# The first superchunk's inverse starts from the corners of its grams, and the second inverse moves behind the front

## The chip, the core and the metric

The kernel runs on one core of one Trainium2 chip. The metric is device time in microseconds, the median of several runs. A core has a matrix engine (TensorE, PE in the rows; PEld is its weight load), a vector engine (VectorE, DVE), an activation engine (ScalarE, ACT), a general engine (GpSimd, POOL) and a queue engine that starts transfers (SyncE, SP). Each works off its own list of instructions in order. They wait for each other by semaphores. SBUF is the memory on the core, PSUM the accumulator memory that TensorE writes, in banks of 128 x 2 KB.

## What is computed

A recurrent attention (delta rule) over 4 x 8 heads, 768 tokens and a head size of 48, and on its output two feed-forward layers, all in float32:

```python
k_n = k / (np.linalg.norm(k, axis=-1, keepdims=True) + 1e-06)
for t in range(768):
    y[:, :, t] = np.einsum('bhd,bhde->bhe', q[:, :, t], state)
    v_old = np.einsum('bhde,bhd->bhe', state, kt)
    state = state + bt[:, :, :, None] * np.einsum('bhd,bhe->bhde', kt, vt - v_old)
x = x @ w_a * (x @ w_b) @ w_out          # 3072 x 384, width 1536
h = x @ w_in                             # width 2048
y = (np.maximum(h, 0) + alpha * np.minimum(h, 0)) @ w_out2
```

## The kernel before

**Attention in chunks.** The 768 tokens are six superchunks of 128 tokens, each two steps (j = 0, 1) of 64. Within a step the recurrence is solved in closed form. The Gram matrix of the keys (`gram_keys`, tile `g`), scaled by b (beta and the key norms) and masked below the diagonal (`mask_keys`, into `ef`), gives a unit triangular 64 x 64 system for each of the 32 head columns of a step, and its inverse is needed. Each 64 x 64 system is cut into 32 x 32 blocks. The two diagonal blocks are inverted on DVE by substitution, all heads and both steps at once: `inverting` does it with 60 operations (a product into `itmp`, an addition into `inv`, 30 times), each pair depending on the pair before. `inverting_halves` does it with 88 operations by 16 x 16 blocks, and ACT hands blocks over between them. `diagonal` then transposes the result with two DVE transposes (`hw`, `TT`), and `offdiag` makes the block beside the diagonal with two sets of 32 x 32 matmuls on PE: `w`, whose results ACT copies into `hw`, and `xx`, whose results ACT copies into `TT`.

**A step.** `step` uses the inverse: `rp` (state times keys; v minus it on DVE), `up` (inverse times v, copied into SU), `sp` (the state's part, subtracted in SU on DVE) and `yp` (the output, which ACT and DVE split into the `x` of the feed-forward). `gram_queries` makes the masked query-key products that `yp` needs; before, ACT copies them out of PSUM (`keep_queries`) and POOL multiplies them with the mask (`mask_queries`). L is the superchunk at hand, N the next one.

**Feed-forward.** Its matmuls are 128 x 512 (3666 in all), float32 in three passes of a rounded format: `p` (up projections), `o` (down projection), and `h` and `o` of the second layer. For every pair of `p`, ACT copies one half out of PSUM (`a<-p`), DVE multiplies the other onto it (`a<-p,a`), ACT rounds it (`g<-a`) and POOL makes the remainder. Weights come as packed words and are decoded on DVE (`raw<-e`, `raw<-e,raw`), ACT (`e<-raw`, `W<-raw`, `wu<-W`) and POOL.

**What sets the order.** The program is recorded first, one operation after another; a list planner then writes the order of each engine from the dependencies, its table of costs and the order of recording. All instructions therefore bear one line, L201, and are told apart by tile names. In the front the attention of superchunk 0 (with the Gram matrices of superchunk 1) runs ahead of the first `p`. There the second inverse (of N) is recorded in small pieces: `early(n)` asks the weight decoding for a piece and, by `leisurely`, the second inverse for one whenever DVE is free. For c = 1 it is finished (`finish(inv)`) and followed by `diagonal` and `offdiag` between pieces of the feed-forward (`run(moe, ...)`). For c of 2 and more the inverse is made by `inverting_halves` at the end of the superchunk before.

## Time and profile before

| | us |
|---|---|
| median of 3 runs | 1021.15 (1020.98 to 1021.97) |
| span of the profiled execution | 1019.1 |
| PE busy in it | 977.5 (96%) |
| DVE, ACT, POOL busy | 610.0, 477.4, 574.7 |
| first big matmul `p` | 81.04 |
| the second superchunk's `rp` | 136.05 |

A timeline row gives the start, the length from the first to the last of a run of like instructions, the engine, the operation as output<-inputs with shapes, the number of instructions, and in brackets the idle time ahead of it with what ended it. A group row gives, behind the bar, busy time and the mean of one in ns, then the engine's idle time just before them. A small float32 matmul has two records in the trace (a set of 64 small matmuls reads x128), a 128x512 matmul one.

### The profile page before, as it was taken

What the parts mean: (1) busy time and instruction counts of PE and PEld (TensorE: products, weight loads), DVE (VectorE), ACT (ScalarE), POOL (GpSimd) and SP (SyncE); (2) the same over time, 40 slices, a digit from 0 to 9 for tenths busy, and PEclk for the clock granted to TensorE, in tenths of its full rate; (3) what the DMA queues carried; (4) which work ended last, traced back from release to release, by engine and by line L of the source; (5) the groups of instructions that cost most, each with busy time, mean ns of one, the idle gap of its engine ahead of it and who ended that gap; (6) DMA issues with size and microseconds to landing.
All of it is one profiled execution on the core that took longest, in us unless ns stands there. A gap on an engine that the chain in (4) does not pass through costs nothing.

```text
span 1019.1 us, 23984 instructions
## 1 busy us (share of the span) xinstructions
PE 977.5 (96%) x9950; PEld 805.1 (79%) x9950; DVE 610.0 (60%) x1232; ACT 477.4 (47%) x955; POOL 574.7 (56%) x512
## 2 busy tenths in 40 slices
...
GB/s 248 190 81 126 138 115 132 40 2 50 110 1 8 74 79 1 18 19 32 17 64 171 178 146 50 32 19 44 1 63 0 1 63 1 32 1 1 32 0 32
DMA packets 26940, 61.41 MB, mean 60 GB/s; under 512 B 4304, under 2 KB 8912, under 8 KB 26832
## 3 DMA queue, kind: packets, MB, share of 16 engines
q1 hardware_dynamic: 26400, 59.50, 19.3%
...
## 4 chain that ended last, share of the span: by engine, by line
PE 91%; DVE 5%; ACT 1%; issue 1%; DMA 1%; SPq 0%; DVEq 0%; POOL 0%; ACTq 0%
PE o L201 34%; PE p L201 29%; PE h L201 19%; PE up L201 2%; PE yp L201 2%; PE g L201 2%; DVE itmp L201 1%; DVE inv L201 1%; PE rp L201 1%; PE sp L201 1%; DMA k<-in_kn_dram 1%; PE xx L201 1%; PE w L201 1%; DVE raw L201 1%; DVE ef L201 0%
## 5 line engine op out<-in xcount | busy, mean ns | idle before, releaser
L201 PE MATMUL p<-x,wu 128*128 128x512 f32 x1296 | 318.0, 394 | 1.4 <-DVE x L201 0.7
L201 PEld LDWEIGHTS p<-x,wu 128*128 128x128 f32 x1296 | 240.2, 188 | 56.2 <-issue 2.4
L201 POOL TENSOR_TENSOR g<-neg,g 128x512 fp32r<-128x512 f32 x95 | 124.3, 1308 | 256.2 <-ACT g L201 255.6
L201 POOL TENSOR_TENSOR wu<-W,wu 128x384 fp32r<-128x384 f32 x195 | 200.3, 1033 | 110.6 <-ACT wu L201 109.0
L201 PE MATMUL h<-x,v 128*128 128x512 f32 x864 | 211.4, 389 | 0.0
L201 PE MATMUL o<-g,v 128*128 128x512 f32 x870 | 211.4, 388 | 0.0
L201 DVE TENSOR_SCALAR neg<-h,al 128x512 f32<-128x512 f32 (+1 forms) x97 | 72.2, 745 | 218.3 <-PE h L201 218.3
L201 ACT CAST g<-neg 128x512 fp32r<-128x512 f32 (+1 forms) x97 | 59.7, 616 | 298.8 <-DVE neg L201 277.3
L201 PEld LDWEIGHTS o<-g,v 128*128 128x128 f32 x870 | 162.5, 188 | 33.4
L201 PEld LDWEIGHTS h<-x,v 128*128 128x128 f32 x864 | 162.2, 188 | 33.7
L201 PE MATMUL o<-g,wu 128*128 128x512 f32 x648 | 165.5, 394 | 0.5 <-DVE TT L201 0.5
L201 ACT CAST wu<-W 128x384 fp32r<-128x384 f32 x216 | 109.9, 513 | 78.7 <-PE p L201 38.2
L201 PEld LDWEIGHTS o<-g,wu 128*128 128x128 f32 x648 | 120.0, 188 | 27.1 <-issue 0.9
L201 POOL TENSOR_TENSOR g<-a,g 128x512 fp32r<-128x512 f32 x71 | 93.3, 1314 | 30.3 <-ACT g L201 30.1
L201 PE MATMUL g<-Z 48*64 48x64 f32 (+1 forms) x1024 | 66.4, 275 | 27.9 <-DVE ef L201 17.9
L201 DVE TENSOR_TENSOR a<-p,a 128x512 f32<-128x512 f32 x72 | 49.3, 685 | 49.8 <-PE p L201 22.4
L201 DVE TENSOR_TENSOR inv<-inv,itmp 128x240 f32<-128x240 f32 (+23 forms) x236 | 69.9, 296 | 10.4 <-ACT eu L201 2.8
L201 PEld LDWEIGHTS g<-Z 48*64 48x64 f32 x1024 | 50.6, 160 | 28.9 <-DVE ef L201 18.2
L201 DVE SCALAR_TENSOR_TENSOR neg<-h,neg 128x512 f32<-128x512 f32 (+1 forms) x97 | 66.5, 686 | 3.3
L201 ACT COPY a<-p 128x512 f32<-128x512 f32 x72 | 42.2, 586 | 44.7 <-PE p L201 41.6
L201 ACT CAST g<-a 128x512 fp32r<-128x512 f32 x72 | 44.7, 620 | 22.5 <-DVE a L201 22.0
L201 POOL TENSOR_TENSOR f<-f,v 128x384 int32<-128x384 int32 x32 | 38.2, 1205 | 6.6 <-DVE v L201 4.0
...
## 6 DMA issues: line engine op xcount, KB each, us to landing
...
```

Of the source, the lines that this page charges most:

```text
L201: getattr(s.engines[op.eng], op.name)(*(real(x) for x in op.a), **{w: real(x) for w, x in op.k.items()})
```

## The change

For superchunk 0, `corners` makes only the 32 x 32 diagonal corners of the key grams, 128 small matmuls into two banks. DVE masks them with a constant (`corner`, -1 above the diagonal, made by POOL at the start) and transposes them into `turned`. `inverting_corners` multiplies by the transposed b in two halves straight into the PSUM room of the inverse, ACT copies each half to SBUF, and the 60 operations follow as before (`substituting`). `sides` makes the blocks beside the diagonal with 64 matmuls; ACT copies them out with the sign, POOL multiplies by b. `first_sides` takes the place of `diagonal` and `offdiag` for superchunk 0: POOL makes the TT copies that ACT made, `w` and `xx` go in the order of j, and their copies are shared between ACT and DVE. In the step, the half of the SU copies of superchunk 0 goes to DVE, and the first subtract from a zero state becomes an ACT activation. The query grams of N are no longer made ahead and masked by POOL; they are made between the parts of the first steps and masked by DVE straight from PSUM. The second inverse is `inverting_halves` (88 operations), recorded behind `columns(xs, L, 1)`, the last `x` of superchunk 0, rather than in pieces through the front. The case c = 1 loses its own branch and uses the numbers in `DIAGONAL` like the others.

```diff
@@ -484,6 +484,14 @@
             )
+        s.corner = cp.tile([128, 32], F32, name="corner")
+        nc.gpsimd.memset(s.corner, -1.0)
+        for q in range(4):
+            sl = slice(32 * q, 32 * q + 32)
+            nc.gpsimd.affine_select(
+                out=s.corner[sl], in_=s.corner[sl], compare_op=ALU.is_gt, fill=0.0,
+                base=0, pattern=[[1, 32]], channel_multiplier=-1,
+            )
         s.TT = ap.tile([128, 2, 16, 64], F32, tag="TT", name="TT")
@@ -661,25 +669,65 @@
             s.spend(ACT, 2.5)
-    def inverting(s, L, room=None):
+    def corners(s, L, tags):
         nc, ap = s.nc, s.ap
+        raw = ap.tile([128, 32, 32], F32, tag="mb", name="raw0", bufs=1)
+        for j, tag in enumerate(tags):
+            Z = L["Z"][j]
+            g = s.bank("g", tag).rearrange("p (i n) -> p i n", n=32)
+            for i in range(16):
+                for x, rows in enumerate((slice(64, 112), slice(0, 48))):
+                    for h in range(2):
+                        at, e = 64 * x + 32 * h, Z[rows, 0, i, 32 * h : 32 * h + 32]
+                        nc.tensor.matmul(g[at : at + 32, i, :], e, e, start=True, stop=True)
+            nc.vector.tensor_tensor(
+                raw[:, 16 * j : 16 * j + 16, :], g, s.corner.unsqueeze(1).to_broadcast([128, 16, 32]), ALU.mult
+            )
+        turned = L["turned"] = ap.tile([128, 32, 32], F32, tag="mk", name="turned", bufs=1)
+        nc.vector.transpose(turned, raw.rearrange("p a t -> p t a"))
+    def sides(s, L, tags):
+        nc = s.nc
+        for j, tag in enumerate(tags):
+            Z = L["Z"][j]
+            g = s.bank("g", tag).rearrange("p (i n) -> p i n", n=32)
+            for i in range(16):
+                for x, rows in enumerate((slice(64, 112), slice(0, 48))):
+                    nc.tensor.matmul(g[64 * x : 64 * x + 32, i, :], Z[rows, 0, i, 0:32], Z[rows, 0, i, 32:64], start=True, stop=True)
+            for x in range(2):
+                sl = slice(64 * x, 64 * x + 32)
+                nc.scalar.activation(L["ef"][sl, 16 * j : 16 * j + 16, 32:64], g[sl], AF.Copy, scale=-1.0)
+        for x in range(2):
+            sl = slice(64 * x, 64 * x + 32)
+            e = L["ef"][sl, :, 32:64]
+            b2 = L["b"].rearrange("p j a -> p (j a)")[sl]
+            nc.gpsimd.tensor_tensor(e, e, b2.unsqueeze(2).to_broadcast([32, 32, 32]), ALU.mult)
+    def inverting_corners(s, L, room):
+        nc, ap = s.nc, s.ap
+        bt = ap.tile([128, 32], F32, tag="bt", name="bt", bufs=1)
+        nc.vector.transpose(bt, L["b"].rearrange("p j a -> p (j a)"))
         a0 = ap.tile([128, 32, 32], F32, tag="eu", name="eu", bufs=1)
-        nc.vector.transpose(a0, L["ef"][:, :, 0:32].rearrange("p a t -> p t a"))
-        s.spend(DVE, 9)
-        yield
-        nc.vector.memset(a0.rearrange("p t s -> p (t s)")[:, 0:1024:33], 1.0)
-        eu = L["eu"] = a0
-        if room is not None:
-            eu = L["eu"] = room
-            nc.scalar.copy(eu, a0)
-        yield
-        tmp = ap.tile([128, 256], F32, tag="itmp", name="itmp", bufs=1)
+        L["eu"] = room
+        flat = room.rearrange("p t s -> p (t s)")
+        for h in range(2):
+            cs = slice(16 * h, 16 * h + 16)
+            nc.vector.tensor_tensor(
+                room[:, :, cs], L["turned"][:, :, cs], bt[:, cs].unsqueeze(1).to_broadcast([128, 32, 16]), ALU.mult
+            )
+            nc.vector.memset(flat[:, 528 * h : 528 * h + 496 : 33], 1.0)
+            nc.scalar.copy(a0[:, :, cs], room[:, :, cs])
+        return s.substituting(a0, room)
+    def substituting(s, a0, eu):
+        nc = s.nc
+        tmp = s.ap.tile([128, 256], F32, tag="itmp", name="itmp", bufs=1)
         for m in range(1, 31):
-            s.spend(DVE, (1.7 if room is not None else 3.0) + (31 - m) * m / 100)
+            s.spend(DVE, 1.7 + (31 - m) * m / 100)
             nt = 31 - m
@@ -763,6 +811,35 @@
             yield
+    def first_sides(s, L):
+        nc, ef, hw, eu = s.nc, L["ef"], s.ap.tile([128, 32, 32], F32, tag="mb", name="hw", bufs=1), L["eu"]
+        TT = s.TT.rearrange("p j i t -> p (j i) t")
+        low, high = (slice(0, 32), slice(64, 96)), (slice(32, 64), slice(96, 128))
+        nc.vector.transpose(hw.rearrange("p a s -> p s a"), eu.rearrange("p t s -> p s t"))
+        nc.vector.transpose(TT[:, :, 32:64].rearrange("p a t -> p t a"), eu)
+        for j in range(2):
+            for sl in low:
+                nc.gpsimd.tensor_copy(TT[sl, 16 * j : 16 * j + 16, 0:32], TT[sl, 16 * j : 16 * j + 16, 32:64])
+        stages = (
+            (low, ef[:, :, 32:64], hw, high, hw, [s.bank("w") for _ in range(2)]),
+            (high, hw, TT[:, :, 32:64], low, TT[:, :, 32:64], [s.bank("xx", "ab") for _ in range(2)]),
+        )
+        for here, left, right, there, to, banks in stages:
+            for j in range(2):
+                for i in range(8):
+                    for q in (2 * j, 2 * j + 1):
+                        for x in range(2):
+                            nc.tensor.matmul(
+                                banks[x][32 * q : 32 * q + 32, 32 * i : 32 * i + 32],
+                                left[here[x], 8 * q + i, :], right[here[x], 8 * q + i, :], start=True, stop=True,
+                            )
+                for q in (2 * j, 2 * j + 1):
+                    for x in range(2):
+                        got = banks[x][32 * q : 32 * q + 32, 0:256].rearrange("p (i n) -> p i n", n=32)
+                        copy = nc.vector.tensor_copy if here is high and x or here is low and j else nc.scalar.copy
+                        copy(to[there[x], 8 * q : 8 * q + 8, :], got)
     def step(s, c, j, L, mates=(), joined=False, wide=False):
@@ -816,7 +893,8 @@
                     at = 64 * (x ^ n)
-                    nc.scalar.copy(SU[x][64 * x : 64 * x + 64, hs, 0:48], ups[n][at : at + 64])
+                    copy = nc.vector.tensor_copy if c == 0 and x else nc.scalar.copy
+                    copy(SU[x][64 * x : 64 * x + 64, hs, 0:48], ups[n][at : at + 64])
                     s.spend(ACT, 1.9)
@@ -834,6 +912,9 @@
                     at, old, new = 64 * (x ^ n), slice(64 - 64 * x, 112 - 64 * x), slice(64 * x, 64 * x + 48)
+                    if st == 0 and x == 0:
+                        nc.scalar.activation(SN[1 - x][new, hs, 0:48], sps[n][at : at + 48], AF.Copy, scale=-1.0)
+                        continue
                     nc.vector.tensor_tensor(SN[1 - x][new, hs, 0:48], SU[x][old, hs, 0:48], sps[n][at : at + 48], ALU.subtract)
@@ -1095,13 +1176,6 @@
             return more
-        def leisurely(inv):
-            while True:
-                if until[DVE] <= now and next(inv, "end") == "end":
-                    return
-                yield
         def finish(b):
@@ -1114,7 +1188,7 @@
             A.load_values(0, L)
-        finish(A.norms(L))
+        finish(A.norms(L, wp.tile([128, 32, 64], F32, tag="late", name="ef0")))
         N = A.load(1)
@@ -1123,26 +1197,20 @@
         A.clear()
-        ef1 = wp.tile([128, 32, 64], F32, tag="late", name="ef1")
-        for jg, tag in zip(HALF, ("ab", "ab", "g", "pre")):
-            A.mask_keys(L, *jg, A.gram_keys(L, *jg, tag))
-            if jg[1]:
-                A.fold(L, jg[0])
+        A.corners(L, ("ab", "ab"))
+        A.sides(L, ("g", "pre"))
         room = p0.tile([128, 32, 32], F32, tag="inv", name="inv")
-        inv = A.inverting(L, room)
-        next(inv)
-        next(inv)
+        inv = A.inverting_corners(L, room)
         A.scale_keys(L)
...
         A.scale_values(L, 1)
-        norms = A.norms(N, ef1, late=True)
+        norms = A.norms(N, late=True)
         next(norms)
...
         finish(inv)
-        finish(A.diagonal(L))
         finish(norms)
@@ -1249,13 +1317,10 @@
         keep = [2 * M2 - 4]
-        idle = iter(())
         def early(n):
...
                 now += 1
-                next(idle, None)
                 if len(left) > 3 * M1 - EARLY:
@@ -1266,15 +1331,15 @@
         spend(POOL, 8)
-        for i, _ in enumerate(A.offdiag(L)):
+        for i in range(2):
             for h in range(2):
...
             early(OFF[i])
+        A.first_sides(L)
+        closed.clear()
         rooms1.append("pre")
-        inv = A.inverting(N, room)
-        idle = leisurely(inv)
         early(OFF[2])
@@ -1282,9 +1347,7 @@
                 if n < 4:
-                    A.keep_queries(N, *HALF[n], A.gram_queries(N, *HALF[n], "ab"))
-                if n in MQ:
-                    A.mask_queries(N, *HALF[MQ.index(n)], None, nc.gpsimd)
+                    A.mask_queries(N, *HALF[n], A.gram_queries(N, *HALF[n], "ab"), nc.vector)
                 n += 1
@@ -1302,18 +1365,12 @@
                 if c == 1:
-                    finish(inv)
-                    diagonal = A.diagonal(L)
-                    now = max(now, until[DVE])
                     background.append(decoding(DEPTH))
                     run(moe, WAIT)
-                    for _ in diagonal:
-                        run(moe, 1)
                     pools["out"] = Pool(rec, second, (p0,), 1, True)
                     going = run(moe, AHEAD) and going
-                else:
-                    for n, _ in enumerate(A.diagonal(L)):
-                        run(moe, DIAGONAL[n])
+                for n, _ in enumerate(A.diagonal(L)):
+                    run(moe, DIAGONAL[n])
                 tag = "chain" if c == 1 else "pre"
@@ -1359,6 +1416,7 @@
                 columns(xs, L, 1)
+                A.inverting_halves(N, "chain")
                 while len(ready) < LEAD:
```

The order shows the moves. **TensorE, the front**, from the first `w` on. Before:

```order
L201 MATMUL w<-hw,ef 32x32 x64
L201 MATMUL g<-Z 64x64 x32
L201 MATMUL xx<-TT,hw 32x32 x64
L201 MATMUL up<-v,TT 64x48 x32
L201 MATMUL sp<-SU,k 48x48 x32
L201 MATMUL yp<-Z,SU 32x64 x64
L201 MATMUL rp<-SU,Z 64x48 x32
L201 MATMUL up<-v,TT 64x48 x32
```

After:

```order
L201 MATMUL w<-hw,ef_118 32x32 x64
L201 MATMUL xx<-TT,hw 32x32 x64
L201 MATMUL up<-v,TT 64x48 x16
L201 MATMUL g<-Z 64x64 x32
L201 MATMUL up<-v,TT 64x48 x16
L201 MATMUL g<-Z 64x64 x32
L201 MATMUL sp<-SU,k 48x48 x32
L201 MATMUL rp<-SU,Z 64x48 x32
```

In the order counts are matmuls. The grams `g` ahead of `w` are left out; the query grams of N, 64 matmuls, now stand in two lots of 32 behind the halves of `up`.

**VectorE, around the first operations of the second inverse.** Before, it begins right behind the transpositions of the first one:

```order
L201 STREAM_TRANSPOSE hw<-inv 128x32x32
L201 STREAM_TRANSPOSE eu<-ef_213 128x1024
L201 STREAM_TRANSPOSE TT<-inv 128x32x32
L201 MEMSET eu 128x32
L201 TENSOR_SCALAR raw<-e 128x384
L201 SCALAR_TENSOR_TENSOR raw<-e,raw 128x384
L201 TENSOR_TENSOR itmp<-inv,eu 128x30
L201 TENSOR_TENSOR inv<-inv,itmp 128x30
```

After, its first products read `gd` and stand around the last three `x`:

```order
L201 TENSOR_SCALAR raw<-e 128x384
L201 SCALAR_TENSOR_TENSOR raw<-e,raw 128x384
L201 TENSOR_TENSOR itmp<-inv,gd 128x28
L201 TENSOR_TENSOR inv<-inv,itmp 128x2x14
L201 TENSOR_TENSOR itmp<-inv,gd 128x52
L201 TENSOR_TENSOR inv<-inv,itmp 128x2x13x2
L201 TENSOR_SCALAR raw<-e 128x384
L201 TENSOR_TENSOR x<-yp,x 128x256 x2
L201 TENSOR_TENSOR itmp<-inv,gd 128x72
L201 TENSOR_TENSOR x<-yp,x 128x256
L201 TENSOR_TENSOR inv<-inv,itmp 128x2x12x3
L201 SCALAR_TENSOR_TENSOR raw<-e,raw 128x384
```

Behind the last `x` in it, up to and with the transposition `hw` of this inverse, come 128 instructions: 83 of the inverse, 35 of the decoding, seven `a`, two subtracts and `hw`.

**TensorE, the `w` of the second superchunk.** Before, with 108 big matmuls ahead of it:

```order
L201 MATMUL o_1330<-g,wu 128x512
L201 MATMUL o_1333<-g,wu 128x512
L201 MATMUL p<-x,wu 128x512 x9
L201 MATMUL w<-hw,ef_213 32x32 x64
L201 MATMUL p<-x,wu 128x512 x9
L201 MATMUL o_1327<-g,wu 128x512
```

After, with 181 ahead of it:

```order
L201 MATMUL o_1448<-g,wu 128x512
L201 MATMUL o_1453<-g,wu 128x512
L201 MATMUL p<-x,wu 128x512
L201 MATMUL w<-hw,ef 32x32 x64
L201 MATMUL p<-x,wu 128x512 x17
L201 MATMUL o_1444<-g,wu 128x512
```

`xx` then stood behind 204 big matmuls and `rp` behind 219; now they stand behind 207 and 216.

## Rows read from the trace of the kernel before

**Rows 1.** The page's first part: busy time, share of the span, instructions.

```profile
PE 977.5 (96%) x9950; PEld 805.1 (79%) x9950; DVE 610.0 (60%) x1232; ACT 477.4 (47%) x955; POOL 574.7 (56%) x512
```

**Rows 2.** Timeline of TensorE, 0 to 100 us: start, length, operation, [idle before <-releaser].

```profile
7.54 6.54 PE L201 MATMUL g<-Z 48*64 48x64 f32 x126 [0.45 <-DMA Z<-in_kt_dram]
...
44.84 3.75 PE L201 MATMUL g<-Z 48*64 48x64 f32 x64 [16.68 <-DVE ef L201]
48.63 1.54 PE L201 MATMUL w<-hw,ef 32*32 32x32 f32 x128
...
60.45 3.65 PE L201 MATMUL up<-v,TT 64*64 64x48 f32 x64 [3.81 <-ACT TT L201]
63.87 2.21 PE L201 MATMUL sp<-SU,k 64*48 64x48 f32 x64
...
72.09 3.65 PE L201 MATMUL up<-v,TT 64*64 64x48 f32 x64 [1.80 <-DVE v L201]
...
81.04 6.38 PE L201 MATMUL p<-x,wu 128*128 128x512 f32 x27 [0.70 <-DVE x L201]
```

**Rows 3.** Timeline of TensorE, 100 to 140 us.

```profile
107.70 1.29 PE L201 MATMUL w<-hw,ef 32*32 32x32 f32 x128
...
113.12 4.24 PE L201 MATMUL p<-x,wu 128*128 128x512 f32 x18
117.20 2.20 PE L201 MATMUL o<-g,wu 128*128 128x512 f32 x9
...
136.05 1.15 PE L201 MATMUL rp<-SU,Z 48*64 48x48 f32 x64
```

**Rows 4.** Timeline of VectorE, 0 to 60 us.

```profile
10.75 0.42 DVE L201 TENSOR_TENSOR b<-b,s 128x32 f32<-128x32 f32 x2
12.89 1.75 DVE L201 TENSOR_REDUCE ss<-ef 128x32 f32<-128x1536 f32 x1 [1.72 <-ACT ef L201]
...
22.16 0.20 DVE L201 TENSOR_TENSOR itmp<-inv,eu 128x30 f32<-128x30 f32 x1 [0.87 <-ACT inv L201]
...
42.91 2.47 DVE L201 TENSOR_TENSOR ef<-g,mb 128x512 f32<-128x512 f32 x4
...
46.55 1.94 DVE L201 STREAM_TRANSPOSE hw<-inv 128x1024 f32<-128x1024 f32 x1
```

**Rows 5.** Groups of VectorE, 79.05 to 88.02 us: busy us, mean ns, idle before.

```profile
L201 DVE TENSOR_TENSOR inv<-inv,itmp 128x184 f32<-128x184 f32 (+7 forms) x8 | 2.2, 280 | 0.1
L201 DVE SCALAR_TENSOR_TENSOR raw<-e,raw 128x384 int32<-128x384 int32 x4 | 2.2, 550 | 0.0
L201 DVE TENSOR_TENSOR itmp<-inv,eu 128x184 f32<-128x184 f32 (+7 forms) x8 | 2.2, 272 | 0.1
L201 DVE TENSOR_SCALAR raw<-e 128x384 int32<-128x384 int32 x3 | 1.6, 548 | 0.0
L201 DVE TENSOR_TENSOR x<-yp,x 128x256 fp32r<-128x256 f32 x3 | 1.2, 419 | 0.0
L201 DVE TENSOR_TENSOR a<-p,a 128x512 f32<-128x512 f32 x1 | 0.7, 681 | 0.0
```

**Rows 6.** Groups of VectorE, 175 to 213 us: an inverse of 88 operations.

```profile
L201 DVE TENSOR_TENSOR inv<-inv,itmp 128x112 f32<-128x112 f32 (+20 forms) x44 | 12.4, 282 | 2.3 <-ACT eu L201 0.5 <-ACT inv L201 0.4
L201 DVE TENSOR_TENSOR itmp<-inv,gd 128x112 f32<-128x112 f32 (+20 forms) x29 | 7.7, 267 | 1.2 <-ACT inv L201 0.3
L201 DVE TENSOR_TENSOR itmp<-inv,eu 128x16 f32<-128x16 f32 (+14 forms) x15 | 4.4, 291 | 0.5
```

**Rows 7.** Timeline of ScalarE, 50 to 140 us.

```profile
55.08 2.11 ACT L201 COPY TT<-TT 32x1024 f32<-32x1024 f32 x2
...
86.16 1.48 ACT L201 ACTIVATE ef<-k 128x1536 f32<-128x1536 f32 x1
...
132.52 3.01 ACT L201 COPY TT<-xx 32x256 f32<-32x256 f32 x8 [0.16 <-PE xx L201]
```

**Rows 8.** Busy time in one stretch of TensorE, with the granted clock (PEclk).

```profile
core 0: us, PE busy (x), PEclk, DMA share, GB/s
72.00:75.70 3.70, 3.61 (x69) 0.50 0.93 254
```

## The prediction

> **What bounds the kernel now.** I read the busy line first, then TensorE's (PE's) timeline from 0 to 140 us, then those of VectorE (DVE) and ScalarE (ACT) beside it. PE is busy 977.5 us, 96% of the span [rows 1]. Nearly all the rest lies ahead of the first big matmul `p` at 81.04: 16.68 us before the key grams at 44.84, 3.81 before the first `up` at 60.45, 1.80 before the second [rows 2]. From 81.04 on the 128x512 matmuls follow one another: 18 of them begin at 113.12 and the next group at 117.20, so 4.08 / 18 = 0.227 us each [rows 3]. So whatever the front wins or loses stands in full at the end, unless PE has to wait later. What sets the front is a chain on DVE: the first inverse's 60 dependent operations begin at 22.16 and end as its transposition `hw` begins at 46.55 [rows 4]; only then can `w`, `xx` and `up` follow.
>
> The second inverse is the point to watch. Before, its 60 operations fill DVE's gaps while the front runs, and its `w` stands behind 108 big matmuls (107.70, [rows 3]), after it was long done. In the new order all its 88 operations lie behind the first steps' outputs `x`, and its `w` stands behind 181 big matmuls. The small matmuls of the old front are two records each in the trace, the big ones one; counts of big matmuls below are from the order.
>
> **Step 1, an earlier start of the first inverse (gain).** In DVE's new order `b` is ready as before, 10.75 + 0.42 = 11.2 [rows 4]; one corner multiply moved ahead of it adds about 0.7 (a 128x512 operation from PSUM: `a` 0.68, [rows 5]), so 11.9. Then the second multiply 0.7, the transpose `turned` 1.95 (as `hw`, 1.94, [rows 4]), the small transpose of b and the two half multiplies, 1.7 together, and the ACT copy of the second half, 2.11 / 4 or about 0.6 by the TT<-TT pair [rows 7]: 16.9, with hand-overs 17.3, against 22.16. That needs the 128 corner grams by 11.9. They start near 7.54; the nearest row by shape is `w` (32x32 tiles), 64 matmuls in 1.54 us, 24 ns each [rows 2], which makes 3.1 us. The 64-column key grams, 63 in 6.54 us or 104 ns each [rows 2], would make 13.3 us, done at 20.9. I take the former, since corner and `w` both write 32-row, 32-column tiles. Gain 4.9 us; by the other end a loss of about 4.
>
> Inside the first inverse two things swap. Four key-mask multiplies (ef of N, 2.47, [rows 4]) go out; the norm of N, a reduce of 1.75 [rows 4] with four small operations of 0.2 to 0.35, comes in, 2.8. So `hw` is transposed at 17.3 + (48.49 - 22.16) + 0.3 = 43.9, where before it was 48.49: gain 4.6.
>
> **Step 2, from hw to the first up (gain).** Before this took 60.45 - 48.49 = 12.0 us. Now `w` begins at once, DVE does TT's transpose (1.9), three key masks (3 x 0.62), four of the copies, a `raw` pair (1.1) and two copies out of `xx`; a copy is 3.01 / 8 = 0.38 on ACT [rows 7] and I put DVE's at the same. That is 1.9 + 1.9 + 1.5 + 1.1 + 0.8 = 7.2: the first `up` at about 51, 9.4 ahead of before.
>
> **Step 3, what stands between up and sp (loss).** The 64 query grams of N, which ran earlier under the first inverse and beside `w`, now stand in two lots of 32 between and behind the halves of `up`. A lot is the size of the 64 records at 44.84, 3.75 us [rows 2]. `up`'s 64 records take 3.65 us at 60.45 as at 72.09 [rows 2], where the granted clock was 0.50 [rows 8], so both are half-clock times. From up to sp it is 3.65 + 2 x 3.75 = 11.2 us where it was 3.42; at full clock half of that. So sp comes at 56.6 to 62.2 instead of 63.87; I take 61, because PE does as little before it as in the row of before. The lead of 9.4 us is down to 3.
>
> **Step 4, from sp to the first p.** Before: 81.04 - 63.87 = 17.2 [rows 2]. Now DVE has 34 operations from the first SU subtract to the last `x`: by the sizes of [rows 5] two subtracts, three query masks and a key mask 3.8, v 1.7, eight raw operations 4.4, the transpose eu 2.0, two SU copies and two subtracts 2.2, six x 2.5, six small ones 1.1; 17.7 in all, behind sp's own 2.2. With some overlap the first p is sp + 17.2 to 19.5, taken as 18.5: P = 79.5 (74 to 82), before 81.04. Gain 1.5.
>
> **Step 5, the second inverse (the large loss).** From the last `x` (0.4 us behind the first p) to the end of the second `hw` DVE has 128 operations in a row. The 88 of such an inverse sum to 12.4 + 7.7 + 4.4 = 24.5 us [rows 6]; 83 of them lie here, 23.5. Beside them: 35 raw operations of 0.55, 19.3; seven `a` of 0.68, 4.8; two SU subtracts 1.1; `hw` 2.2. Sum 50.9 us. Neighbours that don't depend on each other overlap a little: in the nine microseconds of [rows 5], a like mix, the durations sum to 10.1 us in 8.97, a ratio of 0.89. That would give 45.3, with no wait at all; waits for ACT's hand-overs (0.5 and 0.4 named in [rows 6]) and the lower share of independent operations speak for more. I take D = 47.5, between 45.3 and 51. PE has 181 x 0.227 = 41.1 us of big matmuls in that time. The `a` multiplies that free PSUM stand in the same queue, so PE waits in pieces behind them, and for the last piece at `w`: 0.4 + 47.5 - 41.1 = 6.8 us in all.
>
> Here the Trainium skill speaks against the change. The rows: 88 operations are 24.5 us busy [rows 6], while 60 operations of the whole form, with as many results, take 24.4 us from 22.16 to 46.55 with 2.5 us of masks among them [rows 4], so some 22. "VectorE: DVE Perf Modes", section "Rules for kernel authors", says for chained operations to minimise their count, not their semaphores. The rows agree; by that rule alone, 28 operations of about 0.2 us more, the loss would be some 2 to 3 us of the 6.8.
>
> **Step 6, from hw to rp (loss).** Before, 96 big matmuls lay between `w` and `xx`; now 26, and 9 rather than 15 from xx to `rp`. PE's own work, with xx put at the 1.29 us of w, is 1.29 + 26 x 0.227 + 1.29 + 9 x 0.227 = 10.5 us [rows 3]. ACT, which copies `w` and `xx`, has more: behind hw come on DVE a raw 0.55 and `a` 0.68, then on ACT g<-a 0.6, ef<-k 1.48, eight hw copies 3.0, three small ones 1.5, after that three more (1.6), the TT<-TT pair 2.11 and eight copies out of xx 3.01 [rows 7]. That is 14.5, less overlaps; C = 13.6 (10.5 to 14.5). The ef<-k of the next superchunk stands ahead of the hw copies, so it is paid in full.
>
> **The sum.** rp = P + 0.4 + D + C = 79.5 + 0.4 + 47.5 + 13.6 = 141.0. Before it was 136.05 [rows 3] behind 219 big matmuls; now it stands behind 216, so the like of it is 136.05 - 3 x 0.227 = 135.4. Difference +5.6 us. Behind rp the orders are alike and PE has no idle time to give any of it back. The profiled span goes from 1019.1 to about 1024.8; the median runs lie 2.05 us above the span, so 1021.15 + 5.6, rounded to **1027.0 us**. All low or all high ends of P, D and C together would be -5 and +12; each at its own end with the others as taken, +0.1 to +9.1.
>
> **The rivals.** (a) The forecast: DVE late with the second inverse, PE waiting 5 to 9 us around w, xx and rp: 1024 to 1030. Chance 0.57.
> (b) The same, and the clock falls too. Behind the 1.80 us wait at 72.09 [rows 2] the granted clock was 0.50, the 1.2 GHz level, for the next 3.7 us [rows 8]; PE had been on short matmuls before it. Pieces of 2 to 3 us of waiting could do that here. While DVE is late a slower PE only uses up its waiting; the piece before rp counts, 3.7 / 2 = 1.9 us, and one more behind it the same: 1029 to 1031, with (a)'s own spread to 1033, chance 0.14. "TensorE: Matmul & The Clock Gate", section "Why this matters for your kernels", warns that idle gaps between bursts of matmuls put the clock back to half; the row at 72.09 agrees.
> (c) About even. If the front keeps half of its lead (P = 77) and D is 45.5, with C = 13, rp is at 135.9: +0.5, 1020 to 1023. Chance 0.12.
> (d) Faster: DVE is not late. One mechanism: the lead of step 2 passes through step 3, because the clock is full between 51 and 57 (sp at 57, P = 74.5), and D stays at 45.3. With C = 13 rp comes at 133.2, 2.2 early; with C at PE's 10.5, 4.7 early: 1016 to 1019. It decides where P + D falls below 122 - for P = 74.5, D under 47.5; for P = 79.5, under 42.5. The lead of 9.4 us speaks for it, the half-clock rows before 64 against. Chance 0.12.
> (e) The change doesn't do what it says: corner grams at the key grams' 104 ns, so that the first inverse starts 4 us later than before rather than 4.9 earlier. All of it goes on top of the rest, 9 us: about 1035. Chance 0.05.
>
> **How the numbers follow.** The likeliest is (a), 1027.0. Some 0.2%, 2.0 us, is about what a measurement of this kernel can tell from no change: faster is below 1019.1, same up to 1023.2. (d) is faster, 0.12, with a little of (c), 0.13; (c) with the edge of (a) 0.12 for the same; the rest, 0.75, slower. The range must leave out no more than 2 in 10: from 1018.5, which drops most of (d), to 1032, which drops (e) and the end of (b).
>
> **What would show it.** Step 1: the first 128x30 product near 17.3 and hw transposed near 44. Steps 2 and 3: first up near 51, sp near 61. Step 4: first p at 79.5. Step 5: PE waits on DVE `a` and hw that sum to 5 to 9 us between 85 and 130, w at 125 to 129, DVE without a gap over the same stretch. Step 6: rp at 139 to 143, behind waits on ACT. A second superchunk's hw that is done before its w comes up would make the forecast wrong, and a first p before 77 would halve it.

## The result, and the profile after

The changed kernel takes **1036.58 us** (median; 1035.75 to 1037.95), the kernel before in the same series 1021.56: a ratio of 1.0148, interval 1.0134 to 1.0162. It is slower, as forecast, but by 15.0 us where the forecast of 1027.0 meant 5.9 us. The profiled execution has a span of 1036.2 us (before 1019.1).

| start of ... (us) | before | forecast | after | after against forecast |
|---|---|---|---|---|
| first product of the first inverse | 22.16 | 17.3 | 27.02 | +9.7 |
| transposition of its `hw` | 46.55 | 42.0 | 51.52 | +9.5 |
| first `up` | 60.45 | 51 | 60.19 | +9.2 |
| `sp` | 63.87 | 61 | 68.08 | +7.1 |
| first big `p` | 81.04 | 79.5 | 88.05 | +8.6 |
| `w` of the second inverse | 107.70 | 127.4 | 135.15 | +7.8 |
| the `rp` behind it | 136.05 | 141.0 | 149.08 | +8.1 |

(`hw` and `w` of the forecast are its 43.9 less the 1.9 of the transposition, and its 79.5 + 0.4 + 47.5.) An error as large as the one at `rp` is there already at the first product. From the first `p` to `rp` the trace has 61.0 us, the forecast had 61.5.

The first rows answer to [rows 1] and [rows 2]: the busy line of the page, then the timeline of TensorE after (start, length, operation, count of records, idle time before it and what ended that).

```profile
PE 981.7 (95%) x10206; PEld 808.2 (78%) x10206; DVE 619.7 (60%) x1280; ACT 467.9 (45%) x942; POOL 572.4 (55%) x515
...
6.46 0.32 PE L201 MATMUL g<-Z 48*32 48x32 f32 x4 [6.46 <-DMA Z<-in_kt_dram]
7.48 3.35 PE L201 MATMUL g<-Z 48*32 48x32 f32 x219 [0.70 <-DMA Z<-in_kt_dram]
16.90 3.19 PE L201 MATMUL g<-Z 48*32 48x32 f32 x128 [6.07 <-issue]
23.92 6.38 PE L201 MATMUL g<-Z 48*32 48x32 f32 x127 [3.82 <-issue]
31.94 7.72 PE L201 MATMUL g<-Z 48*64 48x64 f32 x162 [1.65 <-issue]
```

A corner matmul is nearly as short as was forecast: 219 records, two to a matmul, in 3.35 us are 31 ns each (24 was taken, 104 by the other end). But behind 4 + 219 = 223 records TensorE stands still for 6.07 us, 33 records short of the last corner gram, and again for 3.82 us behind the next 128. Both stands are put down to "issue": nothing that the profile shows was waited for. The next rows are the corner path on VectorE, which answers to [rows 4], then ScalarE over the same stretch.

```profile
10.24 0.63 DVE L201 TENSOR_TENSOR raw<-g,corner 128x512 f32<-128x512 f32 x1
...
17.62 0.69 DVE L201 TENSOR_TENSOR raw<-g,corner 128x512 f32<-128x512 f32 x1 [5.37 <-PE g L201]
...
26.92 0.07 DVE L201 MEMSET inv<- 128x16 f32 x1 [4.95 <-ACT eu L201]
27.02 0.20 DVE L201 TENSOR_TENSOR itmp<-inv,eu 128x30 f32<-128x30 f32 x1
```

```profile
19.36 1.19 ACT L201 ACTIVATE ef<-g 32x512 f32<-32x512 f32 x2 [6.31 <-PE g L201]
25.03 1.20 ACT L201 ACTIVATE ef<-g 32x512 f32<-32x512 f32 x2 [4.49 <-PE g L201]
26.26 0.59 ACT L201 COPY eu<-inv 128x512 f32<-128x512 f32 x1
```

Each stand is on the chain. VectorE waits 5.37 us for the second half of the corners. Then the copies `eu`, which the first product needs, stand on ScalarE behind the side copies `ef<-g`, and those wait for sides that TensorE computes behind its second stand. What arrives in the stands is seen in the DMA answers of two short stretches, 13.9 to 16.9 and 21.3 to 24 us (packets of a queue, MB, and their time as a share of the 16 DMA engines'; q1 has the loads, which fill that time). The last line is that of the whole page.

```profile
q1 hardware_dynamic: 200, 0.61, 103.0%
q8 instruction: 1, 0.02, 2.9%
...
q1 hardware_dynamic: 226, 0.65, 103.7%
q8 instruction: 1, 0.02, 2.6%
...
q8 instruction: 80, 1.31, 0.6%
```

From 6.5 to 13.9 and from 16.9 to 21.3 queue q8 has no packet. These two, of 16,384 bytes, begin at 14.06 and 21.43 and take 1.41 and 1.11 us; TensorE goes on 1.4 us behind the end of each. A record has a weight load beside it (both x10206 in the page), so 128 records are 256 instructions; in one packet that is 64 bytes each. The 80 packets of the whole run would hold 20,480 such instructions, and TensorE has 2 x 10,206 = 20,412 (before: 78 packets, 19,900 instructions), so q8 carries TensorE's.

From the first `p` on, TensorE's timeline answers to [rows 3]:

```profile
88.05 6.55 PE L201 MATMUL p<-x,wu 128*128 128x512 f32 x27 [1.54 <-DVE itmp L201]
96.88 2.33 PE L201 MATMUL p<-x,wu 128*128 128x512 f32 x9 [2.27 <-DVE a L201]
...
130.01 2.37 PE L201 MATMUL p<-x,wu 128*128 128x512 f32 x9 [1.32 <-ACT a L201]
...
135.15 1.29 PE L201 MATMUL w<-hw,ef 32*32 32x32 f32 x128 [0.50 <-DVE hw L201]
...
149.08 1.52 PE L201 MATMUL rp<-SU,Z 48*64 48x48 f32 x64 [2.75 <-ACT TT L201]
150.54 2.76 PE L201 MATMUL p<-x,wu 128*128 128x512 f32 x6
```

Steps 5 and 6 are here as forecast: pieces of waiting for VectorE's `a` and `hw`, one of 1.32 us for ScalarE's `a`, and the last one before `rp` for ScalarE. Behind `rp` six big matmuls take 2.76 us, twice what [rows 3] has. The windows (busy and records, PEclk, DMA) show the clock:

```profile
146.00:148.00 2.00, 0.33 (x2) 1.00 0.00 0
148.00:150.00 2.00, 0.84 (x40) 1.00 0.38 77
150.00:152.00 2.00, 2.00 (x44) 0.69 0.56 171
152.00:154.00 2.00, 2.00 (x26) 0.50 0.52 154
154.00:156.00 2.00, 2.00 (x41) 0.96 0.00 0
```

TensorE was busy 1.17 of the 4 us before the clock fell. The lag of 13.7 us at `rp` (149.08 less the like of before, 135.4) grows by 2.3 to 16.0 at the 401st big matmul (211.21 against 195.16) and stays so to 520 us. The share of the clock that the windows lack is 0.31, 0.50 and 0.04 of 2 us each, 1.7 us in all (an estimate), so most of the 2.3 is the clock's. The last 1.1 us of the span's 17.1 come piece by piece behind that, and I have no cause for them. The profiled execution, 1037.95, is the slowest of its four; the medians are 15.0 apart.

### The profile page after: what moved, and what is told of

The parts are those of the page before. It is cut to its first block, busy times and chain, and to the rows that moved or that the text cites. A ratio compares the mean times of both kernels' runs of the same rounds, so it can differ in the third digit from the quotient of the medians.

```text
span 1036.2 us, 24522 instructions
## 1 busy us (share of the span) xinstructions
PE 981.7 (95%) x10206; PEld 808.2 (78%) x10206; DVE 619.7 (60%) x1280; ACT 467.9 (45%) x942; POOL 572.4 (55%) x515
## 4 chain that ended last, share of the span: by engine, by line
PE 83%; POOL 1%; DMA 0%; ACT 0%; issue 0%; DVEq 0%; DVE 0%; ACTq 0%
PE o L201 32%; PE p L201 25%; PE h L201 19%; PE yp L201 2%; PE g L201 1%; PE up L201 1%; PE rp L201 1%; PE sp L201 1%; PE xx L201 0%; PE w L201 0%; DMA raw<-in_w_o_dram 0%; POOL wu L201 0%; POOL W L201 0%; POOL g L201 0%; POOL v L201 0%
## 5 line engine op out<-in xcount | busy, mean ns | idle before, releaser
L201 POOL TENSOR_TENSOR wu<-W,wu 128x384 fp32r<-128x384 f32 x195 | 200.8, 1035 | 119.9 <-ACT wu L201 117.9
L201 PE MATMUL g<-Z 48*64 48x128 f32 (+2 forms) x1280 | 68.9, 268 | 18.8 <-issue 11.5
L201 DVE TENSOR_TENSOR inv<-inv,itmp 128x72 f32<-128x72 f32 (+18 forms) x250 | 72.2, 289 | 11.3 <-ACT eu L201 3.5
L201 PEld LDWEIGHTS g<-Z 48*64 48x64 f32 (+1 forms) x1280 | 53.2, 158 | 19.6 <-issue 12.0
L201 DVE TENSOR_TENSOR itmp<-inv,gd 128x112 f32<-128x112 f32 (+20 forms) x145 | 38.5, 266 | 6.5 <-ACT inv L201 2.4
```

What stands on the lines that cost most here:

```text
L201: getattr(s.engines[op.eng], op.name)(*(real(x) for x in op.a), **{w: real(x) for w, x in op.k.items()})
```

## The experiments

Theory A: TensorE has no instructions. The first 223 records are there, then each 128 come with one packet, and the packets come late among the loads of keys, values and weights. Rival B: the corner form itself is slow, as in rival (e). Behind both: is the rest of the forecast right once the start is early? The runs, with the starts in us:

| run | median (lowest to highest) | ratio, interval | first product | `hw` | first `p` | second `hw` | `rp` |
|---|---|---|---|---|---|---|---|
| before | 1020.9 to 1021.6 by series | | 22.16 | 46.55 | 81.04 | 88.02 | 136.05 |
| after | 1036.58 | 1.0148 | 27.02 | 51.52 | 88.05 | 132.88 | 149.08 |
| pairs | 1035.08 (1034.69 to 1035.32) | 1.0134, 1.0117 to 1.0151 | 24.32 | 48.34 | 84.43 | 128.88 | 145.95 |
| hold | 1038.50 (1035.71 to 1040.00) | 1.0166, 1.0148 to 1.0183 | 26.53 | 50.57 | 86.59 | 130.40 | 147.04 |
| hold2 | 1038.76, one run | | 24.89 | 51.89 | 88.73 | 133.18 | 149.84 |
| full | 1034.30 (1033.06 to 1036.55) | 1.0130, 1.0115 to 1.0146 | 25.40 | 48.86 | 85.17 | 129.89 | 146.48 |
| direct | 1039.64 (1038.46 to 1040.94) | 1.0180, 1.0165 to 1.0195 | 21.00 | 52.56 | 88.99 | 133.46 | 150.08 |
| pairs_direct | 1033.80 (1032.09 to 1036.12) | 1.0124, 1.0107 to 1.0141 | 16.72 | 47.68 | 83.61 | 128.07 | 144.99 |
| full_direct | 1037.94 (1037.13 to 1038.17) | 1.0162, 1.0147 to 1.0177 | 24.50 | 50.11 | 86.51 | 130.98 | 148.16 |
| pairs_direct_dve | 1034.15 (1033.45 to 1035.23) | 1.0131, 1.0114 to 1.0148 | 17.39 | 48.59 | 84.11 | 128.46 | 145.30 |
| direct_dve | 1037.43 (1035.64 to 1039.00) | 1.0159, 1.0144 to 1.0174 | 21.83 | 51.76 | 87.36 | 131.86 | 148.95 |
| norms_dve | 1038.45 (1037.07 to 1038.75) | 1.0167, 1.0152 to 1.0182 | 26.76 | 51.61 | 88.72 | 133.73 | 150.78 |
| nonorm | 1035.85 (1034.83 to 1038.48) | 1.0152, 1.0135 to 1.0169 | 29.25 | 51.36 | 86.69 | 131.13 | 147.74 |
| pairs_direct_nonorm | 1032.02 (1029.67 to 1036.40) | 1.0111, 1.0084 to 1.0139 | 17.18 | 43.28 | 78.33 | 124.10 | 140.34 |
| drop30 | 1032.56 (1031.27 to 1032.93) | 1.0109, 1.0094 to 1.0124 | 26.24 | 50.73 | 84.88 | 125.27 | 143.31 |
| front_only | 1043.62 (1043.09 to 1044.82) | 1.0222, 1.0205 to 1.0239 | 27.58 | 54.28 | 99.92 | 106.28 | 156.93 |
| second_only | 1038.00 (1036.95 to 1038.90) | 1.0163, 1.0148 to 1.0178 | 24.37 | 46.49 | 97.30 | 118.11 | 153.92 |
| pairs_direct_nonorm_drop30 | 1029.05 (1028.08 to 1030.07) | 1.0074, 1.0058 to 1.0091 | 17.51 | 42.72 | 80.49 | 121.42 | 139.43 |

### Why the first inverse starts late: pairs, hold, hold2, full

**pairs**, the corner matmuls over two heads' columns, so half as many (it leaves the corners of every other head out):

```diff
-            for i in range(16):
+            for i in range(0, 16, 2):
...
-                        at, e = 64 * x + 32 * h, Z[rows, 0, i, 32 * h : 32 * h + 32]
-                        nc.tensor.matmul(g[at : at + 32, i, :], e, e, start=True, stop=True)
+                        at, e = 64 * x + 32 * h, Z[rows, 0, i : i + 2, 32 * h : 32 * h + 32]
+                        nc.tensor.matmul(g[at : at + 32, i : i + 2, :], e[:, 0], e, start=True, stop=True)
```

> The changed kernel, but each corner matmul takes the columns of two heads at once (32 x 64), so that 64 matmuls write what 128 wrote; the corners of every other head come out wrong. The changed kernel's TensorE stood for 6.07 us with nothing named at 10.8, after 224 records. Theory A (instruction supply: TensorE has used up the instructions it holds, 224 records, and the next block comes late): corners (128 records) end before the limit, so the second corner multiply on VectorE comes at about 12 instead of 17.6, the stand moves into the side grams, the first product comes at about 20 instead of 27.0, the time falls by 5 to 8 us to about 1030. Theory B (the 32-column corner shape itself makes TensorE stand): fewer of them, the stand shrinks in proportion or stays in the corners; the multiply at 14 to 17. If the time stays at 1036, the first inverse was not what made the kernel 9 us slower than forecast.

TensorE's timeline of this run:

```profile
7.23 4.98 PE L201 MATMUL g<-Z 48*32 48x64 f32 x219 [0.52 <-DMA Z<-in_kt_dram]
17.14 6.37 PE L201 MATMUL g<-Z 48*32 48x32 f32 x127 [4.93 <-issue]
```

The stand is again behind 4 + 219 records, now in the middle of the sides, when the corners are long done: it goes by the number of records. B falls. The first product came at 24.3 and not near 20, since the copies `eu` still queue behind the side copies on ScalarE (the second ends at 23.38), and the second superchunk's reduce (1.73 us) stands ahead of the product. Of the 2.7 us won there only 1.5 are in the time, where 5 to 8 were expected.

**hold** and **hold2** leave the work as it is and start the second superchunk's loads and the first weights later, by a one-column copy on GpSimd ahead of each load, from the first norms (hold) or from the transposed corners (hold2):

```diff
+            if late is not None:
+                nc.gpsimd.tensor_copy(t, late[sl, 0:1])
...
-        N = A.load(1)
+        N = A.load(1, L["n"])
```

> The changed kernel, but the loads of the second superchunk (keys, queries) and the first weights wait for the key norms of the first one (one-element copies on GpSimd into their destinations), so that the DMA engines have less to move before about 12 us. Theory A with the DMA engines as cause: the block of instructions that came in the DMA rows at 14.06 to 15.47 comes 3 us or more earlier, TensorE's stand of 6.07 us at 10.8 falls below 3, the second corner multiply comes before 15. If blocks come at a rate of their own whatever the DMA traffic (theory A2), or the shape is the cause (theory B), the stand stays near 6. Time: by A some 2 to 6 us less than 1036.6, unless the later weights cost it again; by the others no gain.

> As hold, but the second superchunk's loads and the first weights wait for the transposed corners, so that between 8 and 15 us only queries and values are moved. If the DMA engines' load sets how late a block of instructions comes, the second block too comes sooner: TensorE's second stand falls from 3.82 below 2, the first stays near 3 or falls. If a block takes its 7 us from one to the next whatever is moved, the second stand stays at 3.8.

In hold the packets begin at 11.21, 18.17 and 26.73, and the first stand is 3.23 us instead of 6.07:

```profile
13.91 3.19 PE L201 MATMUL g<-Z 48*32 48x32 f32 x128 [3.23 <-issue]
```

Its second stand is still 3.82. In hold2 they begin at 12.98, 16.68, 20.70 and 24.87: 3.7 to 4.2 us apart where the changed kernel has 7.4 and 8.1. TensorE's timeline of hold2:

```profile
15.57 3.20 PE L201 MATMUL g<-Z 48*32 48x32 f32 x128 [5.34 <-issue]
19.30 6.80 PE L201 MATMUL g<-Z 48*32 48x32 f32 x161 [0.53 <-issue]
32.77 0.44 PE L201 MATMUL g<-Z 48*64 48x64 f32 x2 [6.66 <-DMA Z<-in_kt_dram]
```

The second stand is down to 0.53 us; the first, whose packet comes among the loads that are left, is still 5.34. From 13.4 to 27 us, when its later packets come, the loads take only 4.3% of the DMA engines' time. So the loads set how late the blocks come. In the time later loads bring nothing. In hold2 the second superchunk's keys are then late themselves, 6.66 us in the last row. In hold `rp` is 2.0 us earlier and the profiled execution, 1035.71, is the fastest of four, but the others take 1038 to 1040, and I have no cause for that.

**full** computes the whole 64x64 key grams (64 matmuls for 64 corners and 64 sides together), and VectorE masks and folds them:

```diff
-        A.corners(L, ("ab", "ab"))
-        A.sides(L, ("g", "pre"))
+        banks = A.corners(L, ("ab", "ab", "g", "pre"))
...
+            g = s.gram_keys(L, j, i8, tag)
+            nc.vector.tensor_tensor(full[:, sl, :], g, corner, ALU.mult)
+            nc.vector.tensor_tensor(raw[:, sl, :], full[:, sl, 0:32], full[:, sl, 32:64], ALU.add)
```

> The changed kernel with whole 64 x 64 key grams, 64 matmuls in place of 128 corners and 64 sides; VectorE masks the corners out of them and adds the two halves. Theory A: no stand of TensorE before the first inverse; the first product comes at about 20 to 21 instead of 27.0, first p at about 82 instead of 88.05, time about 1030. Theory B: the same, so this run tells what the cure is worth rather than the cause. Rival: if first p stays at 88, something else in the front is as late.

No stand is left ahead of the first inverse, but the product is only at 25.40. VectorE's timeline shows a new loss:

```profile
19.01 3.18 DVE L201 TENSOR_TENSOR inv<-turned,bt 128x512 f32<-128x512 f32 x1
```

The same multiply takes 0.70 in the changed kernel. Beside it GpSimd runs `k<-k,b`, and the multiply ends 0.56 us behind that:

```profile
18.87 2.76 POOL L201 TENSOR_TENSOR k<-k,b 128x1536 f32<-128x1536 f32 x1 [8.20 <-issue]
```

This is 2.5 of the 4.4 to 5.4 us by which the product missed the expected 20 to 21; the second superchunk's reduce stands ahead of the product here too.

The kernel before shows the same limit. Its first stop for "issue" stands behind 2 + 126 + 64 + 2 + 155 = 349 records, which is 223 + 126:

```profile
19.27 6.28 PE L201 MATMUL g<-Z 48*64 48x64 f32 x155 [0.58 <-DMA Z<-in_qt_dram]
26.88 1.27 PE L201 MATMUL g<-Z 48*64 48x64 f32 x35 [1.33 <-issue]
```

### Whether an early start reaches the end: direct, pairs_direct and their variants

In **direct** VectorE writes both copies of the half multiplies itself, so that the first product no longer waits for ScalarE; **pairs_direct** does this on pairs and takes both stands off the path, **full_direct** on full.

```diff
-            nc.scalar.copy(a0[:, :, cs], room[:, :, cs])
+            nc.vector.tensor_tensor(
+                a0[:, :, cs], L["turned"][:, :, cs], bt[:, cs].unsqueeze(1).to_broadcast([128, 32, 16]), ALU.mult
+            )
```

> The changed kernel, but VectorE writes the SBUF copy of the scaled corners itself with two more multiplies, so that no copy of ScalarE stands between the corners and the first product; complete computation. In the changed kernel VectorE waited 4.95 us there for a copy that stood behind the side copies on ScalarE, whose second half waited for TensorE's second stand. Theory A (two stands of TensorE for want of instructions, the first before the last corners, the second before the last sides, both on the chain): the first stand remains, the second leaves the chain; first product at about 23.5 instead of 27.0, first p 3 us earlier, time about 1033. If the copies were late for another reason, the gain at the first product is the same but the first p stays.

> Both at once: each corner matmul takes two heads' columns (half the corners come out wrong), and VectorE writes the SBUF copy itself. Theory A: neither stand is on the chain; first product at 17.5 to 18.5, where the forecast had put it (17.3), first p at 79 to 81 (forecast 79.5), rp at 140 to 142 (forecast 141.0), time 1027 to 1029. If the time stays above 1031 although the first product comes at 18, then the forecast's other steps hid an error of their own.

> Whole 64 x 64 key grams, 64 matmuls in place of 192, and VectorE writes the SBUF copy itself; complete computation. First product at 21 to 22.5, first p 83 or earlier, time 1030 to 1032 by theory A: better than the changed kernel, and worse than the one before, since the late second inverse costs its 6 to 7 us whatever the front does.

The first product comes at 27.02 with both stands ahead of it, at 21.00 in direct with the first alone, and at 16.72 in pairs_direct, where the forecast had 17.3: the arithmetic of Step 1 was right without the stands, though with half the corner matmuls and no copy on ScalarE. But the time is 1033.80, only 2.8 us less than the changed kernel's, and `hw` is at 47.68, not 42. Its VectorE timeline says why:

```profile
42.59 0.24 DVE L201 TENSOR_TENSOR itmp<-inv,eu 128x84 f32<-128x84 f32 x1
46.27 0.18 DVE L201 TENSOR_SCALAR r<-r 128x32 f32<-128x32 f32 x1 [3.43 <-POOL r L201]
```

The second superchunk's norm stands inside the first inverse; four of its operations go by GpSimd and come there behind eight query masks. In direct the same wait is 4.65 us: its product came 6.0 us earlier than the changed kernel's, its `hw` 1.0 later, and its time, expected at about 1033, is 1039.64. In full_direct two multiplies stretch beside GpSimd (3.18 and 2.39 us), and its time, expected at 1030 to 1032, is 1037.94.

**pairs_direct_dve**, **direct_dve** and **norms_dve** (the changed kernel with this edit alone) put the norm wholly on VectorE:

```diff
-        norms = A.norms(N, late=True)
+        norms = A.norms(N)
```

> As pairs_direct (half the corners wrong, SBUF copy by VectorE), and the norms of the second superchunk wholly on VectorE, without GpSimd. In pairs_direct the first product came at 16.72, as the forecast had it, yet hw only at 47.68: VectorE waited 3.43 us for a norm step of GpSimd that stands behind GpSimd's eight query masks, and those behind the query grams. Theory C (this coupling is what takes up the front's gain once the stands are off the chain): without it hw begins at 44 to 45.5, first p at 80 to 81.5, time 1.5 to 3.5 us below pairs_direct's 1033.8. If hw stays at 47 or the time does, another wait takes its place.

> Direct with the norms on VectorE; complete computation. Direct had its first product at 21.00 (6 earlier than the changed kernel) but hw at 52.56, 1 later, with 4.65 us of waiting for GpSimd. Theory C: hw at 48 to 49.5, first p 3 us before direct's 88.99, time 1035 to 1037 against direct's 1039.6.

> The changed kernel with the second superchunk's norms wholly on VectorE and nothing else; complete computation. There the wait for GpSimd is only 0.7 us, since VectorE itself comes late. Theory C: less than 1 us either way, the first product still at 27, hw near 51, time 1035 to 1038. If it gains over 2 us, GpSimd was the cause in the changed kernel and not TensorE's stands.

The wait is gone and little is won. From the product to `hw` it takes 31.2 us in pairs_direct_dve (pairs_direct 31.0) and 29.9 in direct_dve (direct 31.6). The time is 2.2 us lower in direct_dve, with ranges that overlap, the same in pairs_direct_dve, and 1.9 higher in norms_dve than in the changed kernel. Rows of pairs_direct_dve, VectorE and then GpSimd:

```profile
44.05 1.28 DVE L201 TENSOR_TENSOR r<-r,s 128x32 f32<-128x32 f32 x1
45.41 1.23 DVE L201 TENSOR_SCALAR r<-r 128x32 f32<-128x32 f32 x1
```

```profile
42.71 5.21 POOL L201 TENSOR_TENSOR Z<-Z,mb 64x512 f32<-64x512 f32 x4
```

Operations on 32 columns, 0.18 to 0.19 alone, take 1.2 to 1.3 while GpSimd's masks (1.3 each) run, and end within 0.05 us of a mask's end. Not every operation does so: a product `itmp<-inv,eu` at 42.97, which reads `inv` from PSUM, takes 0.21 beside the first mask, and a RECIPROCAL at 46.71 takes 0.34 beside the last, neither more than elsewhere.

**nonorm** and **pairs_direct_nonorm** leave the second superchunk's norm out:

```diff
-        norms = A.norms(N, late=True)
-        next(norms)
+        N["n"] = N["b"].rearrange("p j a -> p (j a)")
+        nc.scalar.mul(N["n"], N["n"], 1 / 48)
...
-        finish(norms)
```

> The changed kernel without the second superchunk's norms (left out as in pairs_direct_nonorm); the corner grams are complete. Its first product stood at 27.02 and hw began at 51.52, 24.5 us later. Theory (here the norms cost little, since the first product is so late that their operands have long been there): first product 26 to 27, hw begins at 48.7 to 50, p at 85 to 86.5, time 1033 to 1035.5. Rival (the norms cost the same several us in any order): hw at 46 or earlier, p before 83, time under 1032.

> Leaves out, beside half of the corner grams as in the run pairs_direct: the second superchunk's norms (a Square and a Sqrt on ScalarE, a reduce and four small operations on VectorE, four small ones on GpSimd); its beta is only multiplied by 1/48. In pairs_direct the first product stood at 16.72, hw began at 47.68, 31.0 us later, where the 60 operations alone took some 22 in the kernel before. Theory (the instruction supply sets the start, and the norms inside the first inverse, by their own 2.8 us, their wait on GpSimd and their stretching beside it, give back most of what an early start wins): first product 16.5 to 17, hw begins at 38.7 to 40.5, the first big matmul p at 75 to 77, rp at 136 to 139, time 1024 to 1027. Rival (it is not the norms: the substitution is slow for another reason, or another operand is late next): hw not before 45, p behind 81, time 1031 or more.

From the first product to `hw` the 60 operations take 22.1 us in nonorm, as forecast from [rows 4]; the changed kernel has 24.5, so the norm costs it 2.4 (forecast 2.8). In pairs_direct the same way takes 31.0. Without the norm it is 26.1, of which two stretched second writes are 4.0. Its VectorE timeline:

```profile
27.67 1.64 DVE L201 TENSOR_TENSOR eu<-turned,bt 128x512 f32<-128x512 f32 x1
...
30.11 2.38 DVE L201 TENSOR_TENSOR inv<-turned,bt 128x512 f32<-128x512 f32 x1
...
43.28 1.91 DVE L201 STREAM_TRANSPOSE hw<-inv 128x1024 f32<-128x1024 f32 x1
```

So the theory holds for the norm, though `hw` missed the expected 38.7 to 40.5, by those writes, and `p`, `rp` and the time missed as well. nonorm itself won nothing in the time, and its product came later (29.25), with its `eu` copies still behind others on ScalarE. With pairs_direct_nonorm the front is near what was forecast, `p` at 78.33 (79.5), `rp` at 140.34 (141.0), though without the norm, which the forecast had in it. The time is nevertheless 1032.0 and not 1027.0. TensorE's timeline and windows from `rp` on:

```profile
140.34 2.34 PE L201 MATMUL rp<-SU,Z 48*64 48x48 f32 x64 [2.73 <-ACT TT L201]
142.61 2.93 PE L201 MATMUL p<-x,wu 128*128 128x512 f32 x6
```

```profile
136.00:140.00 4.00, 1.61 (x7) 1.00 0.01 2
140.00:142.00 2.00, 1.66 (x52) 0.58 0.61 197
142.00:144.00 2.00, 2.00 (x27) 0.50 0.22 57
144.00:146.00 2.00, 2.00 (x20) 0.50 0.44 148
146.00:148.00 2.00, 2.00 (x45) 0.71 0.18 43
```

After a stretch in which TensorE was busy 1.61 of 4 us the clock is at half for some 7 us. The lag grows from 5.0 at `rp` to 8.8 at the 401st big matmul: 3.8 us, of which the windows put 3.4 down to the clock by the same estimate. Rival (b) had priced 1.9 twice.

### Whose the loss behind `p` is: drop30, front_only, second_only, pairs_direct_nonorm_drop30

**drop30** leaves the last 30 operations of the second inverse out, **pairs_direct_nonorm_drop30** does so on pairs_direct_nonorm:

```diff
-        for m in range(15):
+        for m in range(0 if tag == "chain" else 15):
```

> The changed kernel without the last 30 of the 88 operations of the second inverse (its blocks beside the diagonal stay unfinished); nothing else is left out. Those 30 sum to about 9 us on VectorE. If VectorE sets the time between the first p and w, as forecast (47 us of VectorE against 41 of TensorE), w follows the first p by 41 to 42 instead of 47.1 us and the time falls by 5 to 6 us to about 1031. If another engine sets it, the time falls by less than 2.

> pairs_direct_nonorm (what that leaves out, this leaves out) that leaves out the last 30 of the 88 operations of the second inverse as well, as in drop30. Theory (front, second inverse and clock add up: drop30 took 4.4 us from p to w): p at 78.3, w at 121 to 122, rp at 136 to 137.5, where the like of before is 135.4; with 0 to 3.5 us for the clock behind rp the time is 1021.5 to 1027. Rival (another wait takes its place: the copies of w and xx on ScalarE stay, and the clock stays at half level as long): rp behind 139, time 1029 or more.

In drop30 `w` comes 42.7 us behind `p` instead of 47.1 (41 to 42 was expected): VectorE sets this stretch, as Step 5 says. The time falls by 4.0, but not all of it is from there. `p` itself comes 3.2 us earlier, 0.8 of it at `hw` already; the planner orders the last steps of the front otherwise. From `p` to `rp` it takes 58.4 us instead of 61.0, only 2.6 less. On the early front it wins little: `p` is 2.2 us later, for a reason that I don't know, `w` comes 43.3 us behind it instead of 48.4, but `rp` is at 139.43, only 0.9 earlier than with the 30 operations. The time is 3.0 lower; the rival's reading (139 or more, 1029) holds. From `w` (123.74) to `rp` it took 15.7 us, 13.7 with them. ScalarE's timeline of this run, and TensorE's `rp`:

```profile
125.53 1.48 ACT L201 ACTIVATE ef<-k 128x1536 f32<-128x1536 f32 x1
...
134.64 2.11 ACT L201 COPY TT<-TT 32x1024 f32<-32x1024 f32 x2
136.77 3.00 ACT L201 COPY TT<-xx 32x256 f32<-32x256 f32 x8
```

```profile
139.43 2.33 PE L201 MATMUL rp<-SU,Z 48*64 48x48 f32 x64 [1.19 <-ACT TT L201]
```

These are pieces that Step 6 summed, one behind the other, and `rp` waits for the copies `TT`, the last of them. Take VectorE's lateness away, and ScalarE's copies are next.

**front_only** is the changed kernel with the second inverse as before: 60 operations in the front's gaps (`inverting` and `leisurely` back).

```diff
+        inv = A.inverting(N, room)
+        idle = leisurely(inv)
         early(OFF[2])
...
-                A.inverting_halves(N, "chain")
```

> The changed kernel with the second inverse made as before: 60 operations, asked for piece by piece through the front. By the order they all stand between the first inverse and the last x on VectorE. If VectorE is full there, the first p moves behind by 10 to 16 us to 98 to 104, while from there to rp TensorE has only its own 52 to 53 us (61.0 in the changed kernel): time 1037 to 1045. If VectorE has room (4.5 us idle between 44 and 88), the first p moves by less than 6 and the time falls to 1030 to 1033.

The first `p` is at 99.92, 11.9 us behind the changed kernel's, so in the new front VectorE has no gaps left for an inverse. From there to `rp` it takes 57.0 us instead of 61.0; the like of before is 54.3. So moving the inverse behind `x` costs 4.0 of the 6.7 us that are lost behind `p`. The other 2.7 are there with the old inverse too, and no run shows their cause.

**second_only** is the kernel before with the second inverse of the change (the reverse of this diff, in the old front).

> The kernel before with the change's second half alone: the second inverse's 88 operations behind the first steps' x, instead of 60 in the gaps of the front; the front is as before, and the computation is complete. Theory (Steps 5 and 6 and the clock behind rp hold by themselves, whatever the front): p at 79 to 81, from p to rp some 61.7 (61.0 in the changed kernel, and three big matmuls more ahead of rp), rp at 140.5 to 143 where it was 136.05, granted clock 0.5 to 0.7 for some 3.5 to 7 us behind it; time 1027.5 to 1031.5. Rival (the loss behind p belongs to the new front, which leaves work over for that stretch): rp at 136 to 138, time 1020.5 to 1023.

This missed both readings, since the planner put the inverse elsewhere: 42 of its operations run between 78.67 and 91.39, ahead of an `x` that the next `yp` waits for. TensorE's timeline:

```profile
91.87 3.64 PE L201 MATMUL yp<-Z,SU 112*32 112x64 f32 x128 [14.48 <-DVE x L201]
```

It says nothing on Steps 5 and 6 by themselves, only what half of these operations cost ahead of an `x`, 14.5 us at one place. Whether the second inverse behind `x` would cost 6.7 us in the old front too stays open.

## Why the prediction was right and wrong

- **The sign** was right, and so was the reason behind it, as far as it goes: late second inverse, TensorE waiting around `w`, `xx` and `rp`. pairs_direct_nonorm, whose first `p` is 2.7 us earlier than before, is still 11.1 us slower. But 7.0 of the 16.0 us come from the front, which had been forecast as a gain of 1.5.
- **Step 1 failed.** The term was a first product at 17.3; it came at 27.02, 9.7 us later, 4.9 behind the kernel before and so beyond even its other end (a loss of about 4). The working priced the corner grams by their length, 24 ns or 104 ns, and was nearly right with the former (31). What it lacked was how 256 short records come to TensorE: 223 are there, the rest waits for a packet among the loads. The timeline of before has a sign of it, at 26.88 us, that I passed over: TensorE stops for "issue" for 1.33 us behind its 349th record (223 + 126). And the corners turn 64 wide matmuls into 128 short ones plus 64 for the sides. The runs pairs (stand behind the same 223 records of another shape), hold and hold2 (later loads, earlier blocks) show the cause; pairs_direct shows the start as forecast without it. It also shows that the start alone doesn't bring the forecast's time back: 2.8 of the 9.6 us by which the time was missed. The next points have the rest.
- **Step 1's second part** (the first inverse from product to `hw`, 24.7) was right as the kernel stands: 24.5. With the early start that was forecast it would have been wrong: 31.0 in pairs_direct. The norm of the second superchunk is not ready then, and leaving it out takes 4.9 off (26.1); the second half's writes, stretched beside GpSimd, are 4.0 of what is left. I had named the reduce and its four operations as 2.8 us of work, not GpSimd's queue behind which they come. So some 6 us of the forecast's gain (47.68 against 42) were not to be had by an early start alone.
- **Step 2** was right: 6.7 us from the end of `hw` (53.45) to `up`, forecast 7.2.
- **Step 3** was too dear: 7.9 us from `up` to `sp`, where 10 was taken, near its half-clock end of 11.2. The granted clock is 0.50 from 53 to 65 us and 0.96 from 65 to 70, so the second lot of query grams ran at nearly full speed. **Step 4** was 1.5 too cheap (20.0, forecast 18.5). Together they gave 0.6 back.
- **Step 5** was right in kind and size: 46.7 us on VectorE (forecast 47.5), busy 43.9 of 46.7 us from 88.5 to 135.2, and TensorE took 47.1 - 41.1 = 6.0 us more than its matmuls need (forecast 6.8). The timeline names 4.5 of that as waits: 3.1 for VectorE's `a` and `hw`, where 5 to 9 was given as the sign, and 1.3 for ScalarE's `a`. drop30 shows that VectorE's operations set the stretch; front_only, that the move of the inverse costs 4.0 of the 6.7 us behind `p`.
- **Step 6** was right: 14.0 us from there to `rp` (13.6), bounded by ScalarE; pairs_direct_nonorm_drop30 shows it as the next bound.
- **Rival (b)** was not a rival but part of the outcome. After `rp` the granted clock is 0.50, the 1.2 GHz level; the lag grew there by 2.3 us, and by 3.8 in pairs_direct_nonorm. The sum put this term at nothing. The pieces of waiting in Steps 5 and 6 had been forecast, and with [rows 8] their price belonged in the sum: with 3.8, and Step 1 as forecast, it is 1030.8, near the 1032.0 that pairs_direct_nonorm took. Rival (e) came near the time, 1035, by a mechanism that pairs excludes; that is luck.
- **Two slips of the working** changed nothing in the forecast. Rival (e)'s own sum, 1027.0 and 8.9 more, is 1036 and not 1035. And 28 operations of 0.2 us are 5.6; the 2 to 3 us in the note to Step 5 are the difference of the busy times, 24.5 and 22.

The lag of the profiled execution at the 401st big matmul is 7.0 (front) + 6.7 (`p` to `rp`) + 2.3 (behind `rp`, mostly the clock) = 16.0 us. No version run here beats the kernel before.
